# Chunked attention and a two-layer MLP on one core: 35 instructions exchange places, q is loaded before v, and the last tile's products are split in halves

## The chip, the cores and the metric

The kernel runs on one NeuronCore of a Trainium2 chip. The core has five engines, each with its own instruction stream that runs strictly in order: PE (TensorE: matmuls, with weight loads shown apart as PEld), DVE (VectorE), ACT (ScalarE), POOL (GpSimd) and SP (SyncE, which here only issues DMAs). They wait for each other through semaphores. The metric is the device time of one execution in microseconds (us).

## The reference

```python
q, k, v: (8, 8, 576, 64) float32            # batch, heads, sequence, head size
scores = scale * q_c @ k_c.T                # in chunks of 64 positions
attn = exp(scores - max); attn /= sum + 1e-9
x = (attn @ v_c) -> (4608, 512)             # tokens x model
h = x @ w_in                                # (512, 2048)
out = max(0.01 * h, h) @ w_out              # (2048, 512), float32
```

## The kernel before

**Tiles.** The 4608 tokens are 36 *units* of 128 tokens (u = 0..35) and 9 *tiles* of 512 tokens (j = 0..8). Unit u's attention makes 128 columns of x, transposed, in `xT`; four units feed one tile of the MLP. Matmuls take fp16 and accumulate in float32 in the eight PSUM banks.

**A unit's attention**, by the names of its tasks and the lines of their instructions:

- load of q and k (L1877, POOL's DMA queue). For the units up to 11 PE transposes them (tq, tk: L2095) and ACT or DVE copies the result to SBUF (q0, q1, k: L1959 on ACT, L1961 on DVE). For the later units SP issues a DMA transpose (L2116) and p0, p1 copy (L1959, L1961).
- s: scores on PE (L2164). m: row maxima (L2170) and b: subtraction (L2173) on DVE. x: exponential on ACT (L2177); h for unit 25. z: row sums on DVE (L2189); ze: + 1e-9 on POOL or DVE (L2192); zi: reciprocal on DVE (L2195); n: product with it on POOL or DVE (L2198).
- e: transpose on PE (L2224) and c: its copy; from unit 20 on d: a DMA transpose (L2232). v: product with v on PE (L2242). a: copy into `xT` on ACT or DVE (L1959, L1961).

**First layer of tile j.** Tiles 0 and 1 are done plainly: L1.j... on PE (L2322) and g, the leaky ReLU, on ACT (L2299). The others use Strassen's scheme with seven products instead of eight, in four parts n = 0..3: xs0.j to xs3.j are sums of blocks of `xT` and fi0 to fi3 sums of blocks of w_in (DVE, L2269); Q1.j.n to Q7.j.n are the products (PE, L2373, four matmuls of 256 columns each). Between them p5.j.n and y.j.n copy out of PSUM or from bank to bank (L1959 or L1961), z.j.n and w.j.n add on DVE (L2398, L2401), and c11, c12, c21, c22 are the leaky ReLU on ACT (L2299). A unit's z has one number behind it, a tile's z has two.

**Second layer of tile j.** Seven products again: S1.j.h to S3.j.h are sums of blocks of the first layer's result (DVE, L2441), S4.j.h.0 a later one (L2536), fo0 to fo3 sums of w_out. P1.j.p0, P1.j.p1 to P7 are the products of the two halves of 128 tokens (PE, L2495, eight matmuls of 256 columns each), in the order P1, P2, P6, P5, P7, P4, P3 as far as their keys go. cp1, cu2, cu3 and d21 copy (L1959 or L1961), d11, d22, d12 add (DVE, L2512) into `osb`, and SP stores (st). P5 and P3 accumulate in one bank, and d22 reads it between them. Tile 8's chain is done for each half apart; its second half has P3 in two parts of 128 columns (L2567) in that same bank, with an add (L2572) and a store (L2557) for each.

**The first loads.** Unit 0's q, k and v come through the hardware queues as whole float32 blocks: v_f and then q_f are issued on SP, k_f on ACT (L1923). castq and castk0, castk1 turn q and k to fp16; put0.0 to put3.0 place v's quarters (all L1959 or L1961).

**Who sets the order.** Nothing is scheduled on the chip. `Plan` (L97 to L280) holds one `Task` per instruction or group, with estimated durations, keys with hand-set offsets (`NUDGE`), buffers from rings (`RINGS`) and, where two engines can do it, a choice of engine. `Plan.run` plays this forward: each engine takes the ready task with the lowest key; buffers and PSUM banks are assigned then. The tasks' `emit` functions are collected in `order` with the planned start, sorted by it, and called in that order. So each engine's stream is the planned order, and each wait is for what was emitted before. Until 24 us idle matmuls (L2608) fill planned gaps on PE.

Of the kernel before, what the change touches and what calls it, by code (L numbers as in the profile page):

```python
# [14 lines left out]
PE, ACT, DVE, POOL, SP = "PE", "ACT", "DVE", "POOL", "SP"  # L15
# [81 lines left out]
class Plan:  # L97
# [89 lines left out]
    def fill(self, a, z, used, count, emit, order):  # L187

        n = count(a, z)
        if not n:  # L190
            return
        for i, o in enumerate(self.rings["bank"]):
            if i not in used and (o is None or not o.open and o.till <= a):
                b = Buf("bank")
                b.till = z + 0.1
                self.rings["bank"][i] = b
                self.whole[i] = False
                order.append((a, emit(n, i)))
                return

    def run(self, slack=0.04, filler=None):
        for t in self.tasks:
            t.left = len(t.deps)
            for d in t.deps:
                d.next.append(t)
        ready = self.ready = {e: [] for e in LATENCY}
        for t in self.tasks:
            if not t.left:
                self.put(t)
        now = dict.fromkeys(LATENCY, 0.75)  # L210
        now[POOL] = 1.25
        order = []
        todo = len(self.tasks)

        def behind(t, e, at):

            return self.lean.get(e, 0.0) + max(now[e], at) + t.engs[e] + sum(x.engs[e] for x in ready[e] if x.key < t.key and x.eng == e)

        while todo:
            best = None  # L220
            for e, ts in ready.items():
                can = []
                loads = []
                for t in ts:
                    if isinstance(t.after, tuple) and t.after[0] == "soft":
                        loads.append(t)
                        continue
                    p = self.place(t, e)
                    if p is None:
                        continue  # L230
                    if len(t.engs) > 1:
                        mine = behind(t, e, p[0])
                        if any(behind(t, o, p[0]) < mine - 1e-9 for o in t.engs if o != e):
                            continue
                    can.append((max(now[e], p[0]), t, p[1]))
                for t in sorted(loads, key=lambda t: t.key):
                    p = self.place(t, e)
                    if p is not None:
                        can.append((max(now[e], p[0]), t, p[1]))
                        break  # L240
                if not can:
                    continue
                first = min(c[0] for c in can)
                wait = self.hold if e in (ACT, DVE) and first < 25.0 else slack
                c = min((c for c in can if c[0] <= first + wait), key=lambda c: c[1].key)
                if best is None or c[0] < best[0]:
                    best = (*c, e)
            ends = self.dma.next()
            if ends and (best is None or ends[0] <= best[0]):
                self.land()  # L250
                continue
            if best is None:
                raise RuntimeError("stuck: " + " ".join(f"{e}:{t.name}" for e, ts in ready.items() for t in ts))
            start, t, slots, e = best
            t.eng = e
            if filler is not None and e == PE:
                self.fill(now[PE], start, [i for b, i in slots if b.ring == "bank"], *filler, order)
            for b, i in slots:
# [6 lines left out]
            order.append((start, lambda t=t: t.emit(t.eng) if len(t.engs) > 1 else t.emit()))  # L265
# [12 lines left out]
        self.now = now  # L278
        order.sort(key=lambda x: x[0])
        return [x[1] for x in order]  # L280


# [1499 lines left out]
           'P3.8.p1': -11.34,  # L1782
           'd12.8.1': 12.97,
           'st.8.1.1': -5.87,
           'st.8.0.1': -12.65},
# [5 lines left out]
 'VROW': (0, 1, 2, 3)}  # L1791

@with_exitstack
def kernel(
# [9 lines left out]
    nc = tc.nc  # L1807

    B, H, S, D = q.shape
    d_model, d_ff = moe_w_in.shape  # L1810
# [51 lines left out]
    def mem(buf):  # L1862
        return MEM[buf.ring][buf.slot]
# [563 lines left out]
    def layer2_seven(j, done):  # L2427
# [45 lines left out]
        def chain(ps_of, k0, span, shift):  # L2473
# [13 lines left out]
            def product(m, deps):  # L2487
                t = []
                opens = m in ("P1", "P2", "P5")
                for p in ps_of:  # L2490
                    def emit(p=p):
                        if opens and p == ps_of[0]:
                            ps[into[m]] = bank(bufs[into[m]], [128, n, HM])
                        for fc in range(HB):
                            nc.tensor.matmul(  # L2495
                                out=ps[into[m]][:, p - ps_of[0], :], lhsT=lhs[m][0]()[:, fc, p * 128:(p + 1) * 128], rhs=rhs[m][:, fc, :],
                                start=(opens and p == ps_of[0] and fc == 0), stop=(fc == HB - 1), skip_group_check=True,
                            )
# [28 lines left out]
            s = side(1)  # L2527
            c22 = dve("d22", "V", tmp(tu3), o(1, 1), key["P7"] + step + 0.2, P5 + [c3], [bV, tu3] + s["bufs"], s["opens"])
            P4 = product("P4", [c3])
            s4 = []  # L2530
            for h in range(2):
# [25 lines left out]
                    f"st.{j}.{name}", SP, 0.5, key["P3"], lambda: nc.sync.dma_start(out=out[r0:r0 + 128, m0:m1], in_=mem(osb[r])[:, 1, m0:m1]),  # L2557
                    deps=deps, bufs=[osb[r]], after=("hard", 0.83 * (m1 - m0) / 512, 1, 0.0))

            leave("ur", 1, HM, d_model, [c22])  # L2560
            leave("ul", 1, 0, HM, [c21])
            leave("l", 0, 0, HM, [c11])
            prev = []
            for q0 in range(0, HM, 128):
                def emit(q0=q0):
                    for fc in range(HB):
                        nc.tensor.matmul(  # L2567
                            out=ps["V"][:, 0, q0:q0 + 128], lhsT=lhs["P3"][0]()[:, fc, 128:256], rhs=rhs["P3"][:, fc, q0:q0 + 128],
                            start=False, stop=(fc == HB - 1), skip_group_check=True)

                def emit_d(q0=q0):
                    nc.vector.tensor_tensor(  # L2572
                        out=mem(osb[0])[:, 1, HM + q0:HM + q0 + 128], in0=ps["V"][:, 0, q0:q0 + 128], in1=mem(tu2)[:, 0, q0:q0 + 128], op=ADD)

                prev = [task(
                    f"P3.{j}.p1.{q0}", PE, 0.46, key["P3"] + 0.01 * q0, emit, deps=[c22] + s4 + lhs["P3"][2] + fo + prev,
                    bufs=lhs["P3"][1] + [bufs["V"]], bank="part")]
                c12 = task(f"d12.{j}.1.{q0}", DVE, 0.2, key["P3"] + step, emit_d, deps=prev, bufs=[bV, tu2, osb[0]])
                leave(f"q{q0}", 0, HM + q0, HM + q0 + 128, [c12])

        if last:
# [29 lines left out]
    for emit in plan.run(filler=(filler, emit_idle)):  # L2611
        emit()


# [28 lines left out]
```

## Time and profile before

| | us |
|---|---|
| median of 3 runs | 282.1 (282.0 to 282.23) |
| the profiled execution | 281.71 |
| its span, first to last instruction | 279.6 |
| PE's first matmul / end of its last | 1.0 / 276.0 |

The profile is of one execution, taken by the hardware. A row of the timeline shows the start and the length in us, the engine and the line, what is written and read, and the number of instructions; a bracket gives the engine's idle time before it and what ended that. Rows with SPq are DMA issues. Granted TensorE clock: 1.0 throughout.

### The profile page before, as it was taken

The numbers are of one execution on the slowest core, as the hardware profiler recorded it, in microseconds if no ns is written. First come the engines' busy times: TensorE is split into PE (matmuls) and PEld (weight loads), VectorE is DVE, ScalarE is ACT, GpSimd is POOL, SyncE is SP. The second block draws the span as 40 slices with busy tenths as digits, with TensorE's granted clock in tenths as the row PEclk, the third lists the DMA queues.
The fourth block names the chain that finished last, engine by engine and source line by source line (L and its number), as shares of the span: only waits on it lengthen the run. The fifth ranks groups of instructions, "written<-read, shape, count | busy, mean of one in ns | idle before, by whom it ended". The sixth has DMA issues, their size and how long they took to land. (4 is left out here: it accounts for less than half of the span.)

```text
span 279.6 us, 8040 instructions
## 1 busy us (share of the span) xinstructions
PE 268.0 (96%) x3249; PEld 242.6 (87%) x3249; DVE 227.3 (81%) x425; ACT 208.1 (74%) x396; POOL 139.1 (50%) x180
## 2 busy tenths in 40 slices
PE   6789999999999989999999999999999999999994
PEld 6778999999988979999889889889889888988884
DVE  5788799989989889899998999878699927734841
ACT  5987999876786899799677897476876766677431
POOL 8979598657876147254736996462334020000000
PEclk9999999999999999999999999999999999999999
DMA  9999999999999939999999999999535022100132
GB/s 147 162 178 164 164 184 193 156 131 122 147 192 180 185 76 124 144 157 175 141 171 138 138 151 173 208 154 172 150 101 108 19 40 80 75 2 0 72 149 81
DMA packets 157236, 37.09 MB, mean 133 GB/s; under 512 B 147600, under 2 KB 152848, under 8 KB 157200
## 3 DMA queue, kind: packets, MB, share of 16 engines
q0 software_dynamic: 113904, 17.96, 98.6%
q1 hardware_dynamic: 42256, 18.36, 39.0%
q8 instruction: 25, 0.41, 0.7%
q10 hardware_dynamic: 1040, 0.26, 0.4%
q14 instruction: 11, 0.09, 0.1%
HBM read 36.70 MB, written 9.44 MB: 165 GB/s over the span
## 5 line engine op out<-in xcount | busy, mean ns | idle before, releaser
L2299 ACT ACTIVATE gT<-bank 128x512 f16<-128x512 f32 x116 | 64.7, 600 | 16.3 <-PE bank L2373 14.7
L2495 PEld LDWEIGHTS <-gT 128*128 128x128 f16 x576 | 55.1, 98 | 6.8 <-issue 0.7
L2495 PE MATMUL bank<-w_outT,gT 128*128 128x256 f16 x432 | 53.7, 273 | 0.5 <-ACT u L1959 0.5
L2373 PEld LDWEIGHTS <-FI 128*128 128x128 f16 x448 | 43.0, 98 | 7.5 <-issue 2.4
L2373 PE MATMUL bank<-xs,FI 128*128 128x256 f16 x336 | 45.7, 272 | 1.5 <-DVE xs L2269 0.6
L2495 PEld LDWEIGHTS <-S 128*128 128x128 f16 x424 | 40.6, 98 | 4.8 <-DVE S L2441 0.3
L1877 POOL DMA_DIRECT2D qk<-in_q_dram x39 | 33.7, 869 | 10.1 <-PE bank L2095 5.3
L1877 POOL DMA_DIRECT2D qk<-in_k_dram x39 | 34.0, 878 | 7.8 <-DMA KT<-qk 5.6
L2495 PE MATMUL bank<-FO,S 128*128 128x256 f16 x288 | 35.7, 273 | 0.0
L2373 PEld LDWEIGHTS <-w_inT 128*128 128x128 f16 x336 | 31.9, 98 | 4.3 <-issue 0.6
L2322 PE MATMUL bank<-xT,w_inT 128*128 128x128 f16 x512 | 32.7, 219 | 0.0
L2373 PE MATMUL bank<-xT,w_inT 128*128 128x256 f16 x224 | 31.3, 273 | 0.0
L2322 PEld LDWEIGHTS <-w_inT 128*128 128x128 f16 x512 | 29.5, 98 | 0.0
L1959 ACT ACTIVATE p<-bank 128x512 f32<-128x512 f32 (+1 forms) x37 | 20.6, 586 | 11.0 <-PE bank L2495 5.5
L2198 POOL TENSOR_TENSOR en<-ex,z 128x512 f16<-128x512 f16 x18 | 20.4, 1138 | 14.6 <-DVE z L2195 5.7
L2192 POOL TENSOR_SCALAR z<-z 128x8 f32<-128x8 f32 x25 | 8.4, 336 | 38.0 <-DVE z L2189 30.7
L2189 DVE TENSOR_REDUCE z<-ex 128x8 f32<-128x512 f16 x36 | 24.4, 678 | 3.4 <-ACT ex L2177 3.1
L2177 ACT ACTIVATE ex<-sh 128x512 f16<-128x512 f32 x35 | 22.1, 631 | 6.4 <-DVE sh L2173 4.6
L2398 DVE TENSOR_TENSOR bank<-bank,p 128x512 f32<-128x512 f32 x28 | 19.0, 694 | 8.7 <-PE bank L2373 6.5
L2170 DVE TENSOR_REDUCE mx<-bank 128x8 f32<-128x512 f32 x36 | 24.4, 681 | 1.8 <-PE bank L2164 1.8
L2173 DVE TENSOR_TENSOR sh<-bank,mx 128x512 f32<-128x512 f32 x35 | 23.6, 679 | 0.5
L2401 DVE TENSOR_TENSOR w<-bank,p 128x512 f32<-128x512 f32 x28 | 18.8, 686 | 5.8 <-PE bank L2373 5.7
(83 smaller groups left out, 478.4 us busy)
## 6 DMA issues: line engine op xcount, KB each, us to landing
out_dram<-osb SPq DMA_DIRECT2D x16, 512.0 KB, 5.1
VB<-in_v_dram POOLq DMA_DIRECT2D x14, 288.0 KB, 8.5
qk<-in_k_dram POOLq DMA_DIRECT2D x31, 128.0 KB, 6.8
qk<-in_q_dram POOLq DMA_DIRECT2D x31, 128.0 KB, 8.5
w_outT<-in_moe_w_out_dram POOLq DMA_DIRECT2D x4, 512.0 KB, 10.2
w_inT<-in_moe_w_in_dram POOLq DMA_DIRECT2D x6, 256.0 KB, 6.5
qk<-in_k_dram POOLq DMA_DIRECT2D x8, 64.0 KB, 6.1
w_inT<-in_moe_w_in_dram POOLq DMA_DIRECT2D x4, 128.0 KB, 6.1
```

The costliest lines, as they stand in the source:

```text
L1877: nc.gpsimd.dma_start(out=to[a - r0:z - r0, which], in_=src[a // S, :, a % S:a % S + z - a, :].rearrange("h p d -> p h d"),)
L1959: nc.scalar.activation(out=to(), in_=of(), func=AFT.Copy, bias=0.0, scale=1.0)
L2170: nc.vector.tensor_reduce(out=mem(mx)[:, 0], in_=t["sp"], axis=AXL.X, op=ALU.max)
L2173: nc.vector.tensor_tensor(out=mem(sh), in0=t["sp"], in1=mem(mx)[:, 0].unsqueeze(2).to_broadcast((128, 8, CH)), op=ALU.subtract)
L2177: nc.scalar.activation(out=mem(ex), in_=mem(sh), func=AFT.Exp, bias=0.0, scale=SCL)
L2189: nc.vector.tensor_reduce(out=mem(z)[:, 0], in_=mem(ex), axis=AXL.X, op=ALU.add)
L2198: (nc.gpsimd if eng == POOL else nc.vector).tensor_tensor(out=mem(en), in0=mem(ex), in1=mem(z)[:, 2].unsqueeze(2).to_broadcast((128, 8, CH ...
L2299: nc.scalar.activation(out=to, in_=of, func=AFT.Prelu, bias=0.0, scale=1.0, alpha=0.01)
L2322: nc.tensor.matmul(out=t["h"][:, i, :], lhsT=w_inT[:, n, fc * 128:(fc + 1) * 128], rhs=xT[:, n, r0 % RING:r0 % RING + tb], start=(i == 0 a ...
L2373: nc.tensor.matmul(out=ps[to][:, i, :], lhsT=lhs[:, t, f:f + 128], rhs=rhs()[:, t], start=(opens and i == 0 and t == 0), stop=(t == 1), sk ...
L2398: nc.vector.tensor_tensor(out=ps["V"], in0=ps["X"], in1=mem(p5), op=ADD)
L2495: nc.tensor.matmul(out=ps[into[m]][:, p - ps_of[0], :], lhsT=lhs[m][0]()[:, fc, p * 128:(p + 1) * 128], rhs=rhs[m][:, fc, :], start=(opens ...
```

## The change

1. `Plan.run` takes a list of moves. After the order is sorted, each pair (a, b) takes task a out and puts it directly ahead of task b. Where a stood behind b, a comes earlier by one to four places on its engine; in some pairs a stood further ahead, so that others pass it. Buffers, banks and engines stay as planned.
2. The list has 36 pairs. The first puts q_f ahead of v_f on SP.
3. In the second half of tile 8, P5 is split into two products of 128 columns as P3 was, each half has a bank of its own from P5 to P3, and d22 and d12 become two adds each.

Applied one after the other, the pairs make these orders on the engines (only stretches that the prediction speaks of):

- SP: q_f, v_f.
- DVE, 28 us: q0.7, then the memset zv.1.1.1. 38 us: z.5, fi2, fi0.
- ACT, 99 us: y.2.3, a.14. PE, 102 us: Q4.2.0, e.12. DVE, 100 us: zi.12, zi.22.
- DVE, 139 us: z.4.0, z.21; then S4.3.0.0, w.4.0, and S4.3.1.0 only ahead of y.4.1.
- PE, 157 us: s.25, v.23, P4.3.p0, P5.4.p0, P4.3.p1. DVE: S3.4.1, m.25, z.26, zi.24, xs0.5, d22.3.0, xs1.5, zi.26, xs2.5, n.26.
- DVE, 195 us: b.31, xs2.6, xs3.6.
- DVE, 213 us: z.32, m.34, S1.6.1, zi.32, S2.6.1, b.34, m.35, S3.6.1, b.35. PE, 217 us: P6.6.p1, P2.6.p1, v.28, P7.6.p0.

```diff
-                order.append((a, emit(n, i)))
+                order.append((a, emit(n, i), None))
...
-    def run(self, slack=0.04, filler=None):
+    def run(self, slack=0.04, filler=None, moves=()):
...
         order.sort(key=lambda x: x[0])
+        for name, behind_it in moves:
+            x = next(x for x in order if x[2] == name)
+            order.remove(x)
+            order.insert(next(i for i, y in enumerate(order) if y[2] == behind_it), x)
         return [x[1] for x in order]
...
+ 'MOVES': (('q_f', 'v_f'),
+           ('P3.1.p0', 'Q3.2.1'),
+           ('zi.12', 'zi.22'),
+           ('a.14', 'c22.2.2'),
+           ('S3.6.1', 'b.35'),
+           ('b.34', 'm.35'),
+           ('m.34', 'zi.32'),
+           ('xs0.5', 'd22.3.0'),
+           ('z.26', 'xs0.5'),
+           ('fi2', 'fi0'),
+           ('q0.7', 'zv.1.1.1'),
+           ('w.4.0', 'S4.3.1.0'),
+           ('z.4.0', 'z.21'),
+           ('xs3.5', 'z.25'),
+           ('S4.3.1.0', 'y.4.1'),
+           ('Q5.5.3', 's.27'),
+           ('zi.24', 'xs0.5'),
+           ('xs2.5', 'n.26'),
+           ('Q4.2.0', 'e.12'),
+           ('xs3.7', 'zi.35'),
+           ('P2.6.p1', 'v.28'),
+           ('v.29', 's.34'),
+           ('P5.4.p0', 'P4.3.p1'),
+           ('P3.3.p0', 'Q1.5.1'),
+           ('L1.1.0.1.0', 'L1.1.1.2.0'),
+           ('P7.5.p0', 'P4.4.p1'),
+           ('b.31', 'xs2.6'),
+           ('c12.7.0', 'c22.7.1'),
+           ('s.32', 'Q2.6.2'),
+           ('Q6.8.0', 'P6.7.p1'),
+           ('Q1.7.2', 'P4.6.p1'),
+           ('y.5.3', 'c11.5.2'),
+           ('Q2.2.2', 'P7.1.p1'),
+           ('m.34', 'S1.6.1'),
+           ('Q3.3.3', 'e.16'),
+           ('y.2.2', 'S4.1.1.0'),)}
...
-            P5 = product("P5", [])
+            apart = n == 1 and ps_of[0] == 1
+            QS = range(0, HM, 128) if apart else ()
+            bW = [Buf("bank") for _ in QS]
+            pw = {}
+
+            def quarter(m, q0, deps):
+
+                i, opens = q0 // 128, m == "P5"
+
+                def emit():
+                    if opens:
+                        pw[i] = bank(bW[i], [128, 128])
+                    for fc in range(HB):
+                        nc.tensor.matmul(
+                            out=pw[i], lhsT=lhs[m][0]()[:, fc, 128:256], rhs=rhs[m][:, fc, q0:q0 + 128],
+                            start=(opens and fc == 0), stop=(fc == HB - 1), skip_group_check=True)
+
+                return task(
+                    f"{m}.{j}.p1.{q0}", PE, 0.46, key[m] + 0.01 * q0, emit, deps=list(deps) + lhs[m][2] + fo,
+                    bufs=lhs[m][1] + ([] if opens else [bW[i]]), opens=[bW[i]] if opens else [], bank="part")
+
+            def add(name, r, q0, by_, key, deps, bufs, opens):
+                def emit():
+                    nc.vector.tensor_tensor(
+                        out=mem(osb[r])[:, 1, HM + q0:HM + q0 + 128], in0=pw[q0 // 128], in1=mem(by_)[:, 0, q0:q0 + 128], op=ADD)
+                return task(f"{name}.{j}.1.{q0}", DVE, 0.2, key, emit, deps=deps, bufs=[bW[q0 // 128], by_] + bufs, opens=opens)
...
+                c22 = [add("d22", 1, q0, tu3, key["P7"] + step + 0.2, P5[q0] + [c3], s["bufs"], s["opens"]) for q0 in QS]
...
+            for q0 in QS:
+                P3 = quarter("P3", q0, [c22[q0 // 128]] + s4)
+                c12 = add("d12", 0, q0, tu2, key["P3"] + step, [P3], [osb[0]], [])
                 leave(f"q{q0}", 0, HM + q0, HM + q0 + 128, [c12])
```

More of the change, by code (lines that the diff above doesn't have):

```diff
@@ L264, in run @@
             now[e] = t.end
-            order.append((start, lambda t=t: t.emit(t.eng) if len(t.engs) > 1 else t.emit()))
+            order.append((start, lambda t=t: t.emit(t.eng) if len(t.engs) > 1 else t.emit(), t.name))
             for o in t.engs:
@@ L1784 @@
            'st.8.1.1': -5.87,
-           'st.8.0.1': -12.65},
+           'st.8.0.1': -12.65,
+           'P5.8.p1.0': 46.8,
+           'P5.8.p1.128': 46.8,
+           'P3.8.p1.0': -11.34,
+           'P3.8.p1.128': -11.34,
+           'd22.8.1.0': 4.69,
+           'd22.8.1.128': 4.69,
+           'd12.8.1.0': 12.97,
+           'd12.8.1.128': 12.97},
  'RINGS': {'osb': 3, 'qk': 5, 'QZ': 2, 'KT': 6, 'QT': 4, 'et': 5, 'p5': 3},
@@ L2523, in chain @@
             c2 = act("cu2", "X", tmp(tu2), key["P6"] + step, P6, [bX], [tu2])
-            P5 = product("P5", [])
+            apart = n == 1 and ps_of[0] == 1
[19 more added lines that the diff above has]
+                return task(f"{name}.{j}.1.{q0}", DVE, 0.2, key, emit, deps=deps, bufs=[bW[q0 // 128], by_] + bufs, opens=opens)
+            if apart:
+                P5 = {q0: [quarter("P5", q0, [])] for q0 in QS}
+            else:
+                P5 = product("P5", [])
             P7 = product("P7", [c2])
             c3 = act("cu3", "X", tmp(tu3), key["P7"] + step, P7, [bX], [tu3])
-            s = side(1)
-            c22 = dve("d22", "V", tmp(tu3), o(1, 1), key["P7"] + step + 0.2, P5 + [c3], [bV, tu3] + s["bufs"], s["opens"])
+            if apart:
+                s = side(1)
+                c22 = [add("d22", 1, q0, tu3, key["P7"] + step + 0.2, P5[q0] + [c3], s["bufs"], s["opens"]) for q0 in QS]
+            else:
+                s = side(1)
+                c22 = dve("d22", "V", tmp(tu3), o(1, 1), key["P7"] + step + 0.2, P5 + [c3], [bV, tu3] + s["bufs"], s["opens"])
             P4 = product("P4", [c3])
@@ L2558, in leave @@
                     deps=deps, bufs=[osb[r]], after=("hard", 0.83 * (m1 - m0) / 512, 1, 0.0))
-            leave("ur", 1, HM, d_model, [c22])
+            leave("ur", 1, HM, d_model, c22)
             leave("ul", 1, 0, HM, [c21])
             leave("l", 0, 0, HM, [c11])
[L2563 to L2578, printed above, removed]
+            for q0 in QS:
+                P3 = quarter("P3", q0, [c22[q0 // 128]] + s4)
+                c12 = add("d12", 0, q0, tu2, key["P3"] + step, [P3], [osb[0]], [])
                 leave(f"q{q0}", 0, HM + q0, HM + q0 + 128, [c12])
@@ L2609, in emit_idle @@
         return go
-    for emit in plan.run(filler=(filler, emit_idle)):
+    for emit in plan.run(filler=(filler, emit_idle), moves=KNOBS.get("MOVES", ())):
         emit()
```

2 lines of the change are left out of this document (1 added, 1 removed).

## The prediction

> **What bounds the kernel now.** I read the busy times first.
>
> ```profile
> PE 268.0 (96%) x3249; PEld 242.6 (87%) x3249; DVE 227.3 (81%) x425; ACT 208.1 (74%) x396; POOL 139.1 (50%) x180
> ```
>
> PE (TensorE) is busy for 268.0 of 279.6 us, so exchanging instructions can win at most the 11.6 us in which it is idle. The table by stretches says where those are.
>
> ```profile
> 0.00:30.00 30.00, 24.70 (x407) 22.62 (x408) 21.75 (x53) 22.62 (x43) 26.67 (x39) 1.00 1.73 163
> ```
> ```profile
> 230.00:280.00 50.00, 45.98 (x447) 41.20 (x444) 26.12 (x47) 25.54 (x49) 0.00 (x0) 1.00 0.18 64
> ```
>
> The columns are stretch, length, then PE, PEld, DVE, ACT and POOL busy with instructions, granted clock, DMA share, GB/s. PE idles 5.3 us in the first 30, 4.0 us in the last 50 (nearly all behind the last product), and so 2.3 us in the 200 us between. There it stops only in short stalls. The chain of waits shows the last of these (start, length, what):
>
> ```profile
> 217.97 0.63 ACT ex L2177
> 218.60 0.49 ACT u L1959
> 219.10 0.04 issue
> 219.14 1.03 PE bank L2495 x8
> 220.17 7.00 PE bank L2373 x64
> ```
>
> From 219.14 the chain is PE to the last product. The last row gives PE's pace: 7.00 / 64 = 0.109 us for a product of 256 columns. A row's own length is longer, because matmuls overlap; so I measure a stall as the start of the waiting product less the start of the one before it plus 0.109 us for each of its matmuls. It is then a little longer than the idle time in the row's bracket.
>
> **The change part by part.** Moves add and remove no work. A move is worth the stall that it ends, less the stall that it opens.
>
> *219 us.* P7.6 waits for cu2.6, a copy on ACT (line 1959).
>
> ```profile
> 217.62 1.04 PE L2495 MATMUL bank<-w_outT,gT 128*128 128x256 f16 x8
> ```
>
> PE was free at 217.62 + 8 x 0.109 = 218.49 and began P7.6 at 219.14: a stall of 0.65. By the chain the copy stood behind x.34 (ACT ex), which waited for b.34 on DVE. The change puts m.34 and b.34 ahead of S3.6.1, so x.34 is over before cu2.6's input exists. S3.6.1, which P7.6 also reads, takes b.34's place behind m.34, b.34 and m.35; it is done no later than b.34 is now, before x.34 begins at 217.97, and so ahead of 218.49. **-0.65.**
>
> *The load of q first.* SP issues v_f's DMA, then q_f's.
>
> ```profile
> 1.25 0.57 SPq L1923 DMA_DIRECT2D u<-in_q_dram  x1
> ```
> ```profile
> 6.69 0.63 ACT L1959 ACTIVATE qk<-u 128x512 f16<-128x512 f32 x1 [2.23 <-DMA u<-in_q_dram]
> 7.34 0.41 ACT L1959 ACTIVATE S<-p 64x256 f16<-64x256 f32 x1
> 7.81 0.59 ACT L1959 ACTIVATE QZ<-bank 64x512 f16<-64x512 f16 x1
> ```
> ```profile
> 9.14 0.40 PE L2095 MATMUL bank<-ident,qk 128*128 128x128 f16 x4 [0.59 <-DVE qk L1961]
> ```
>
> The second of the two lands just before 6.69. After the change that one is v. The cast of q (6.69) then goes early, but the next instruction in ACT's order, put2.0 (7.34), reads v: it starts near 6.69, not earlier. Behind it stand q1.0 (7.81), then q0.0 and castk0 on DVE, then tk.0 on PE (9.14) and all of unit 0. So of ACT's 2.23 us of waiting for q only 7.34 - 6.69 = 0.65 comes out at the end of this chain. Bounds: 0, if v lands 0.65 later than q did; 2.2, the whole wait, if v lands with q. I take the row at which v's place in the queue is now filled. **-0.65.** It lasts only if the next loads are there 0.65 earlier too (second rival).
>
> *q0.7 ahead of a memset.*
>
> ```profile
> 27.57 0.30 DVE L1977 MEMSET VB<- 64x288 uint32 x1
> 27.90 0.42 DVE L1961 COPY QZ<-bank 64x512 f16<-64x512 f16 x1
> ```
> ```profile
> 29.67 0.39 PE L2164 MATMUL bank<-KT,QZ 128*128 128x64 f16 x8 [0.24 <-ACT gT L2299]
> ```
>
> ACT waits for this copy, does q1.7 and then g.0.0.0, which frees the bank that s.7 opens at 29.67. All of it starts 27.90 - 27.57 earlier: **-0.33.** The memset's reader is far off.
>
> *fi2 behind z.5.* e.5 waits for n.5 on POOL.
>
> ```profile
> 42.89 0.40 PE L2224 MATMUL bank<-ident,en 128*128 128x128 f16 x4 [0.22 <-POOL en L2198]
> ```
>
> z.5 goes ahead of a long sum, but its input x.5 ends behind n.4, so DVE waits a little; n.5 still meets fi1. Between -0.4 (the stall with what the bracket hides) and +0.4: I take **+0.1.**
>
> *Around 100 us.* Q6.2.3 waits for y.2.3, ahead of which a.14 goes away; e.12 waits for n.12.
>
> ```profile
> 99.69 1.03 PE L2373 MATMUL bank<-xs,FI 128*128 128x256 f16 x8 [0.56 <-ACT bank L1959]
> ```
> ```profile
> 101.73 0.40 PE L2224 MATMUL bank<-ident,en 128*128 128x128 f16 x4
> 101.96 0.60 PE L2373 MATMUL bank<-xs,w_inT 128*128 128x256 f16 x4
> ```
> ```profile
> 100.76 0.69 DVE L2401 TENSOR_TENSOR w<-bank,p 128x512 f32<-128x512 f32 x1
> ```
>
> The earlier y.2.3 does not come through: w.2.0 (100.76) is behind z.2.0 and n.22 on a full DVE, and Q4.2.0 needs it. Q4.2.0, now ahead of e.12, can start at 101.45 + 0.04, e.12 follows, and what came behind Q4.2.0 starts 0.23 + 0.44 later, at 102.16 in place of 102.40. **-0.24**; between 0 and -0.6, the whole first bracket.
>
> *140 us.* z.4.0 and w.4.0 each go ahead of one DVE instruction.
>
> ```profile
> 138.00 1.91 PE L2495 MATMUL bank<-FO,S 128*128 128x256 f16 x16
> 140.08 0.60 PE L2373 MATMUL bank<-xs,FI 128*128 128x256 f16 x4 [0.16 <-DVE bank L2398]
> ```
> ```profile
> 141.82 0.60 PE L2373 MATMUL bank<-xT,w_inT 128*128 128x256 f16 x4
> 142.47 0.60 PE L2373 MATMUL bank<-xs,w_inT 128*128 128x256 f16 x4
> ```
>
> The stalls are 140.08 - 139.74 = 0.34 and 142.47 - 142.26 = 0.21, each shorter than the instruction of about 0.6 that is passed. What is passed (z.21, S4.3.1.0) has readers microseconds later. **-0.55**, or 0 if DVE brings the wait back.
>
> *160 us.* Q5.5.2 waits for xs0.5.
>
> ```profile
> 156.96 1.04 PE L2495 MATMUL bank<-FO,S 128*128 128x256 f16 x8
> 157.84 0.40 PE L2242 MATMUL bank<-et,VB 128*128 128x64 f16 x8
> 158.07 1.91 PE L2495 MATMUL bank<-FO,gT 128*128 128x256 f16 x16
> 160.61 0.27 PE L2373 MATMUL bank<-xs,FI 128*128 128x256 f16 x1 [0.62 <-DVE xs L2269]
> ```
> ```profile
> 157.01 0.59 ACT L1959 ACTIVATE u<-bank 128x512 f32<-128x512 f32 x1
> ```
> ```profile
> 159.55 1.00 DVE L2269 TENSOR_TENSOR xs<-xT 128x512 f16<-128x512 f16 x1
> 160.48 0.41 DVE L2269 TENSOR_TENSOR xs<-xT 128x512 f16<-128x512 f16 x1
> ```
> ```profile
> 159.23 1.04 POOL L2198 TENSOR_TENSOR en<-ex,z 128x512 f16<-128x512 f16 x1
> ```
>
> The stall is 160.61 - 159.81 = 0.80. xs0.5 goes ahead of d22.3.0, to 159.0, and so ahead of POOL's n.24; alone such a sum takes 0.41. But P5.4.p0 (156.96) is also moved, between P4.3's two halves. v.23 then takes its place and ends at 157.19, and P4.3 must wait for cu3.3.0 on ACT until 157.60: a **new stall of 0.43** that P5.4.p0 covered, with P5.4.p0, P4.3.p1 and Q5.5.2 queued behind it. **-0.37**, between +0.1 and -0.8.
>
> One page speaks against this place. The Trainium skill, "SBUF — State Buffer", Who interferes with whom, says that a DVE instruction with two SBUF inputs and a POOL instruction that reads SBUF exclude each other, and that the first to issue blocks the other. The trace agrees: xs0.5 began behind n.24 and took 1.00. By that rule this term is -0.37 if xs0.5 issues first and about nothing if n.24 does.
>
> *199 us.* b.31 goes ahead of two sums; x.31, p5.6.1, z.6.1 and Q7.6.1 hang on it.
>
> ```profile
> 198.43 0.60 PE L2373 MATMUL bank<-xT,w_inT 128*128 128x256 f16 x4
> 199.10 0.38 PE L2373 MATMUL bank<-xs,FI 128*128 128x256 f16 x2
> ```
>
> 199.10 - 198.87 = **-0.23**, or 0.
>
> *The last products by halves.* P5 and P3 get a bank for each half; the matmuls cost the same.
>
> ```profile
> 276.02 0.49 DVE L2572 TENSOR_TENSOR osb<-bank,u 128x128 f32<-128x128 f32 x2 [1.27 <-PE bank L2567]
> ```
> ```profile
> 276.34 0.33 SPq L2557 DMA_DIRECT2D out_dram<-osb  x1
> 276.76 0.38 SPq L2557 DMA_DIRECT2D out_dram<-osb  x1
> ```
>
> Now both adds wait until P3's second half is done, and two stores then queue on SP. With its own bank the first half's add and store run under the second half, and the last store goes in the slot of the first: 276.76 - 276.34 = **-0.42.** Nothing lies behind it. The cost is one more add for d22, covered by P4 (0.87 on PE).
>
> The other moves meet stalls of about 0.1 or none. I set their gains against new waits like P5.4.p0's, and count neither.
>
> The sum: 0.65 + 0.65 + 0.33 - 0.10 + 0.24 + 0.55 + 0.37 + 0.23 + 0.42 = 3.34. The profiled execution took 281.71 (span 279.6 and 2.1 around it), the median is 282.1, 0.4 above. 282.1 - 3.3 = **278.8 us.**
>
> **The rivals.**
>
> *The waits come back one place further on.* Against a full gain: DVE is 81% busy on the mean; a product that is early finds the next sum unfinished. For the gain: DVE's own idle times there are waits for PE, which shrink with it. If the terms at 28, 100, 140, 160 and 199 us (1.72) are lost, 1.62 is left: 280.5.
>
> *The loads hold the start.*
>
> ```profile
> DMA  9999999999999939999999999999535022100132
> ```
>
> The DMA engines have work nearly all the time until slice 14. If landings, not PE, set the pace there, what is won before 30 us (0.65 + 0.33) is lost again: 279.8. Against it: units wait microseconds behind their loads.
>
> *Slower: DVE and POOL fall out of step.* Every move shifts which of DVE's two-input sums meets a POOL instruction. The price is 1.00 - 0.41 = 0.59 each (the rows at 160 us). It decides when more than 3.34 / 0.59, so six, new meetings stand directly before a product that waits; with eight the time is 278.8 + 4.7 = 283.5. Against it: POOL works only half the time, and between 30 and 230 us few stalls end on such a sum. The rule behind it is that of the Trainium skill, "SBUF — State Buffer", Who interferes with whom; the price is the rows'.
>
> *The order does not do what it says:* a wait on an engine's count may still cover the instruction that was passed, as both last adds now wait for the second half. For the last tile that costs 0.42: 279.2, inside the forecast.
>
> **How the numbers follow.** Forecast 0.63 (with the fourth rival), waits that return 0.19, loads 0.12, slower 0.04, about no change 0.02. About 0.2% (0.56 us) is what a measurement can tell from no change. Faster 0.94, same 0.02, slower 0.04. The low end adds to 3.34 the 0.43 of the new stall, 0.5 if e.5's wait goes, 0.4 of the first bracket at 100 us and 0.2 of the bounds of q's load: 277.2. The high end takes in most of the first rival: 280.7.
>
> **What would show it.** Right: tk.0 near 8.5; no idle before Q7.4.0, Q4.4.0, Q7.6.1 and P7.6; a new idle before P4.3 at about 157 less the shift; d12's first add beginning under P3's second half. Wrong: put2.0 not at v's landing; the same brackets one product later; sums of 1.0 us in new places.

## The result, and the profile after

The changed kernel took 278.19 us (median of 4 runs, 277.98 to 278.58), the kernel before 282.17 on the same chip (4 runs, 282.0 to 282.3): a ratio of 0.9863, interval 0.9848 to 0.9878. The forecast was 278.8 in a range of 277.2 to 280.7. The profiled execution is the slowest of the four, 278.58 with a span of 276.6; against the profile of before (281.71, 279.6) that is 3.1 less, between the medians 4.0. The two differ because the profile of before is of a faster execution than its median and this one is of the slowest; where executions of one kernel differ, the experiments show in part.

The busy times, first view of the page of the changed kernel:

```profile
PE 267.6 (97%) x3257; PEld 242.9 (88%) x3257; DVE 226.7 (82%) x426; ACT 207.9 (75%) x396; POOL 139.1 (50%) x180
```

No work went away (eight matmuls and one add more, from the halves). TensorE's idle time went from 11.6 us to 9.0. Where it went, the table by stretches shows (columns as in the prediction), cut at the start of P1.0.p0, the first product of tile 0's second layer, and at the start of P3's second half, the last product. Before:

```profile
30.00:58.11 28.11, 27.89 (x531) 27.73 (x528) 26.71 (x43) 26.23 (x51) 20.83 (x27) 1.00 2.00 174
58.11:275.37 217.26, 214.80 (x2311) 191.78 (x2309) 178.34 (x328) 159.15 (x305) 91.56 (x116) 1.00 1.28 124
275.37:279.60 4.23, 0.61 (x11) 0.44 (x8) 0.49 (x2) 0.14 (x1) 0.00 (x0) 1.00 0.29 93
```

After:

```profile
0.00:30.00 30.00, 25.37 (x416) 23.19 (x417) 22.97 (x54) 23.18 (x43) 26.36 (x39) 1.00 1.75 165
30.00:57.94 27.94, 27.48 (x522) 27.30 (x520) 26.39 (x43) 25.58 (x50) 19.93 (x26) 1.00 1.99 168
57.94:272.67 214.73, 214.11 (x2320) 192.00 (x2318) 176.70 (x329) 158.97 (x305) 92.78 (x117) 1.00 1.29 126
272.67:276.60 3.93, 0.61 (x11) 0.43 (x8) 0.58 (x2) 0.13 (x1) 0.00 (x0) 1.00 0.32 100
```

The second column is the length. The **middle** went from 217.26 to 214.73, 2.53 less; the **end** from 4.23 to 3.93, 0.3 less; the **start** only from 58.11 to 57.94, 0.17 less, though the forecast had put 0.88 there (0.65 + 0.33 - 0.10).

In the middle the waits that the prediction wanted to end are gone; Q6.2.3, from which it took nothing, still stalls for 0.45 (0.73 before). Where the chain of waits had its last stall, with ACT's ex and u, it now reads:

```profile
211.08 5.24 PE bank L2543 x48
216.55 0.87 PE bank L2543 x8
217.43 7.00 PE bank L2421 x64
```

It runs on TensorE alone now. The timeline at Q7.4.0, Q4.4.0 and Q7.6.1 (start, length, what; an idle time would stand in a bracket) has no bracket left:

```profile
139.15 0.60 PE L2421 MATMUL bank<-xs,FI 128*128 128x256 f16 x4
...
141.34 0.60 PE L2421 MATMUL bank<-xs,w_inT 128*128 128x256 f16 x4
...
197.06 1.47 PE L2421 MATMUL bank<-xs,FI 128*128 128x256 f16 x12
```

The start went as forecast, and then not. tk.0 is at 8.30 (9.14 before), and 0.63 to 0.64 of that holds up to v.2, the product at 22.56 (23.19 before). Then come these two rows, L1.0.0.1.0 and e.3:

```profile
23.43 0.34 PE L2370 MATMUL bank<-xT,w_inT 128*128 128x128 f16 x3 [0.31 <-DMA w_inT<-in_moe_w_in_dram]
...
27.55 0.40 PE L2272 MATMUL bank<-ident,en 128*128 128x128 f16 x4 [0.36 <-ACT QZ L2007]
```

The first waits for loadQ.2.1, which landed at 23.39 (at 22.71 before). The second had no bracket before; e.3 stood at 27.51 then, so nothing of the gain was left there. q0.7's place gave 0.5 back at s.7 (29.20, 29.67 before), and e.5 took 0.25 of that (its stall is 0.63, 0.38 before).

At the end the first half's add starts at 272.87, under the second half's product, which began at 272.67 and ends at 273.28. This is as planned:

```profile
272.22 1.06 PE L2585 MATMUL bank<-w_outT,S 128*128 128x128 f16 x16
...
272.87 0.29 DVE L2595 TENSOR_TENSOR osb<-bank,u 128x128 f32<-128x128 f32 x1 [1.03 <-PE bank L2585]
273.31 0.29 DVE L2595 TENSOR_TENSOR osb<-bank,u 128x128 f32<-128x128 f32 x1 [0.15 <-PE bank L2585]
```
```profile
273.25 0.38 SPq L2639 DMA_DIRECT2D out_dram<-osb  x1
```
```profile
273.73 0.40 SPq L2639 DMA_DIRECT2D out_dram<-osb  x1
```

From the end of the last matmul (273.28) to the start of the last store (273.73) 0.45 us pass; before, 276.76 - 275.98 = 0.78.

### The profile page after: what moved, and what is told of

The parts are those of the page before. It is cut to its first block, busy times and chain, and to the rows that moved or that the text cites. A ratio compares the mean times of both kernels' runs of the same rounds, so it can differ in the third digit from the quotient of the medians.

```text
span 276.6 us, 8050 instructions
## 1 busy us (share of the span) xinstructions
PE 267.6 (97%) x3257; PEld 242.9 (88%) x3257; DVE 226.7 (82%) x426; ACT 207.9 (75%) x396; POOL 139.1 (50%) x180
## 4 chain that ended last, share of the span: by engine, by line
PE 81%; DMA 9%; POOL 5%; ACT 1%; DVE 1%; issue 1%; POOLq 0%
PE bank L2543 38%; PE bank L2421 30%; PE bank L2370 6%; DMA VB<-in_v_dram 4%; DMA w_inT<-in_moe_w_in_dram 3%; PE bank L2290 3%; PE bank L2212 2%; DMA qk<-in_k_dram 2%; POOL qk L1925 2%; PE bank L2272 1%; POOL xs L2093 1%; PE bank L2143 1%; PE bank L2585 1%; DVE xs L2317 1%; ACT ex L2225 0%
## 5 line engine op out<-in xcount | busy, mean ns | idle before, releaser
L2543 PEld LDWEIGHTS <-S 128*128 128x128 f16 x416 | 39.7, 98 | 4.7 <-DVE S L2489 0.3
L2543 PE MATMUL bank<-FO,S 128*128 128x256 f16 x280 | 34.8, 273 | 0.0
L2240 POOL TENSOR_SCALAR z<-z 128x8 f32<-128x8 f32 x25 | 7.5, 301 | 32.7 <-DVE z L2237 26.7
L2007 ACT ACTIVATE xT<-bank 128x512 f16<-128x512 f32 x36 | 21.2, 599 | 3.0 <-PE bank L2290 2.8
```

Of the source, the lines that this page charges most:

```text
L2007: nc.scalar.activation(out=to(), in_=of(), func=AFT.Copy, bias=0.0, scale=1.0)
L2543: nc.tensor.matmul(out=ps[into[m]][:, p - ps_of[0], :], lhsT=lhs[m][0]()[:, fc, p * 128:(p + 1) * 128], rhs=rhs[m][:, fc, :], start=(opens ...
```

## The experiments

Theory going in: each stall on TensorE is a term of its own, and the terms add up. Rivals: landings of loads set the pace before 60 us; a removed wait comes back one place further on. All times are medians; each ratio is against the kernel before on the same chip, whose median was 281.9 to 282.2. Starts and stalls are worked out as in the prediction, each from one profile of the kernel in question. The medians of the kernels that have most of the moves lie between 277.96 and 279.24, and most of their intervals overlap; so what a single move is worth is read from the traces.

**The halves alone.**

```
-         'MOVES': (('q_f', 'v_f'), ... ),}
+         'MOVES': ()}
```

> The changed kernel without any of its 36 moves: only the last tile's products by halves are left. Theory (the end is a step of its own, nothing upstream of it matters): every product up to the last starts when it did before, and from the end of the last matmul to the start of the last store 0.45 to 0.36 us pass in place of 0.78, so the time is 0.33 to 0.42 us under that of before, about 281.8. Rival (the order does not do what it says, a wait on a count still covers what was passed): 0.78 stays and the time is 282.2.

281.61, ratio 0.9986 (0.9975 to 0.9996), 0.38 under the kernel before. From the last matmul to the last store 0.45 passes, as in the changed kernel. The theory holds at its lower end: by the trace the halves are worth 0.33.

**Only the moves with a term of their own.** The list of moves is cut to these:

```
+ 'MOVES': (('q_f','v_f'), ('a.14','c22.2.2'), ('S3.6.1','b.35'), ('b.34','m.35'), ('m.34','zi.32'),
+           ('xs0.5','d22.3.0'), ('fi2','fi0'), ('q0.7','zv.1.1.1'), ('w.4.0','S4.3.1.0'),
+           ('z.4.0','z.21'), ('Q4.2.0','e.12'), ('P5.4.p0','P4.3.p1'), ('b.31','xs2.6'))}
```

> The changed kernel with 13 of its 36 moves, those that the forecast gave a term of their own (q_f, q0.7, fi2, a.14, Q4.2.0, z.4.0, w.4.0, xs0.5, P5.4.p0, b.31, b.34, S3.6.1 and the first move of m.34), and the halves. Theory of the forecast (the other 23 are worth nothing together): the time of the full change, 278.2 within 0.3. Rival read from the two traces (y.2.2 and Q2.2.2 are worth 0.20 at 88 us, two more places 0.07 and 0.06): 278.5. Second rival (the 23 guard against waits that the 13 open): 279 or more.

279.2, ratio 0.9899 (0.9883 to 0.9915): the second rival. From P1.0.p0 to the last product it takes 215.96, against 214.73 with all moves and 217.26 with none. So the thirteen are worth 1.30 there, and the other 23 another **1.2**. The places differ by 0.35 at 89 us, 0.27 at Q4.4.0, 0.15 at v.20 just behind it and 0.39 from there to Q2.5.1, with a small rest. In the last of these one sees how a small move works. s.27 waits for p0.27, a copy on POOL, in this run:

```profile
159.07 1.47 PE L2398 MATMUL bank<-xs,FI 128*128 128x256 f16 x12
160.01 0.65 POOL L1986 COPY QZ<-QT 64x512 f16<-64x512 f16 x1
160.72 0.41 PE L2189 MATMUL bank<-KT,QZ 128*128 128x64 f16 x8 [0.17 <-POOL QZ L1986]
160.96 0.60 PE L2398 MATMUL bank<-xs,FI 128*128 128x256 f16 x4
```

TensorE is free at 159.07 + 12 x 0.109 = 160.38 and loses 0.34. The product behind it, Q5.5.3 (160.96), could have gone; one of the 23 moves puts it ahead of s.27, and in the changed kernel s.27 (160.65) has no bracket.

**The old order of q's and v's loads.**

```
- 'MOVES': (('q_f', 'v_f'),
+ 'MOVES': (
```

> The changed kernel, with v's load ahead of q's on SP as it was before; the other 35 moves stay. Theory of the forecast (the 0.65 won at tk.0 goes through to the end): tk.0 at 9.1 in place of 8.3, and 278.85. Rival (the loads set the pace until 24 us): tk.0 is 0.8 later, but L1.0.0.1.0, which waits for loadQ.2.1's landing, starts within 0.2 of the changed kernel's 23.43, and the time is 278.2 to 278.4.

278.7, ratio 0.9889 (0.9871 to 0.9906). tk.0 is at 9.14, v.2 at 23.20, 0.64 behind the changed kernel; L1.0.0.1.0 at 23.59 is 0.16 behind it, as the rival says, and e.3 stands where it did. But later this execution lost 0.45 at e.5 and another 0.5 at tq.8:

```profile
54.92 0.40 PE L2142 MATMUL bank<-ident,qk 128*128 128x128 f16 x4 [0.37 <-DMA qk<-in_q_dram]
```

From P1.0.p0 (58.96) to the last product it takes 214.72, the changed kernel's 214.73. So the middle repeats to 0.01, and what is uncertain lies before 58 us. The time decides nothing: 278.7 is what neither side said, and the changed kernel itself has 278.19 in one set of runs and 278.53 in another (next).

**The changed kernel again.**

> The changed kernel itself once more, on the chip on which the next three run, so that they can be set against it. Expected: 278.2, and from 60 us on the same starts relative to each other as in its first profile (P1.0.p0 to the last product within 0.05), while the stalls before 60 us differ by some tenths, as those of kernels with the same order there did.

278.53, ratio 0.9881 (0.9865 to 0.9896). On this chip the change is worth 3.4 (281.91 to 278.53), in the first set of runs 4.0; its five executions lie between 277.99 and 279.15, and the profiled one is the fastest of them. The middle takes 214.85, 0.12 more, where 0.05 was expected (all between Q2.5.1 and P2.5.p0). The start is 0.7 shorter than in the first profile of the very same program. P1.0.p0 in the first profile and in this one:

```profile
57.94 0.82 PE L2543 MATMUL bank<-w_outT,gT 128*128 128x256 f16 x6
```
```profile
57.23 0.82 PE L2543 MATMUL bank<-w_outT,gT 128*128 128x256 f16 x6
```

Two waits make the difference. L1.0.0.1.0 has none:

```profile
22.96 0.61 PE L2370 MATMUL bank<-xT,w_inT 128*128 128x128 f16 x8
```

And e.3 is at 26.88 in place of 27.55. In both profiles it starts 0.05 after n.3's end on DVE (27.50 and 26.83). The bracket of the first names ACT's copy q0.5, which ended at 27.50 too; but in the second q0.5 ends at 27.20, behind e.3's start, so it isn't what e.3 needs. n.3 hangs on ze.3, a sum of 128x8 on DVE that was caught behind a DMA issue of POOL's in the first profile:

```profile
24.55 1.16 POOL L1937 DMA_DIRECT2D VB<-in_v_dram  x1
24.86 0.85 DVE L2240 TENSOR_SCALAR z<-z 128x8 f32<-128x8 f32 x1
25.70 0.89 POOL L1925 DMA_DIRECT2D qk<-in_k_dram  x1
```

and slipped in just behind the start of the next issue in the second:

```profile
23.56 1.16 POOL L1937 DMA_DIRECT2D VB<-in_v_dram  x1 [0.21 <-issue]
24.70 0.89 POOL L1925 DMA_DIRECT2D qk<-in_k_dram  x1
24.87 0.17 DVE L2240 TENSOR_SCALAR z<-z 128x8 f32<-128x8 f32 x1
```

Of the kernel before such a pair exists too: the halves alone have its order up to there, and e.3 is at 27.99 (ze.3 took 0.62) against 27.51 (0.17).

So against the one profile of before the start is worth 58.11 - 57.94 = 0.17 by the first profile and 58.11 - 57.23 = **0.88** by the second. That the second is the forecast's 0.88 is chance: in the profile of the halves alone, which has the order of before, P1.0.p0 is at 58.59, and against that the two give 0.65 and 1.36.

**Can the start's gain be held by order?** Three runs. In all three n.5 is issued before zi.5, so it reads the reciprocals that an earlier unit left in the same buffer (unit 7, by the planned buffers) in place of unit 5's; e.5's wait for zi.5 is then missing from their times. To the changed kernel's list the first adds:

```
+           ('loadQ.2.1','loadQ.4.1'), ('loadQ.4.1','loadk.7'), ('zi.3','zv.1.1.0'), ('n.3','zv.1.1.0'),
+           ('q1.5','zv.1.1.3'), ('q0.5','zv.1.1.3'), ('n.5','loadq.11'),
```

> The changed kernel and seven further moves at the three stalls that gave the start's gain back: loadQ.2.1 and loadQ.4.1 exchange places in POOL's order (L1.0.0.1.0's stall of 0.47); zi.3 and n.3 go ahead of two memsets on DVE, q1.5 and q0.5 ahead of one on ACT (e.3's stall of 0.53); n.5 goes ahead of loadq.11's issue on POOL (e.5's stall of 0.63). Theory (these waits, and not PE's work, swallowed what q's early load had won): 1.3 to 1.6 less, 276.7; L1.0.0.1.0 near 23.0, e.3 near 26.7, e.5 near 41.0. Rival (the DMA engines, busy nearly all the time, hold the next products instead): the waits come back at tq.5, tq.7, tq.4 or s.6, and 277.6 or more.

278.97, ratio 0.9896 (0.9876 to 0.9915). L1.0.0.1.0 at 22.67, e.3 at 26.40 and e.5 at 41.69 are all early, the last by 1.0 against the first profile. By e.6 it is gone:

```profile
45.84 0.83 PE L2377 MATMUL bank<-xT,w_inT 128*128 128x128 f16 x12 [0.40 <-DVE sh L2228]
```

L1.1.1.2.0 waits for b.6, which stands on DVE behind the long sum fi3. With 0.32 more two products on, e.6 is at 49.86 (49.83 in the changed kernel). The rival's time came, but its reason was wrong: DVE's order, not a landing. The second run adds:

```
+           ('zv.1.1.0','q1.4'), ('zv.1.1.2','q1.4'), ('zv.1.1.1','q1.4'),
+           ('loadq.11','loadq.10'), ('loadk.15','loadq.13'), ('m.6','fi3'), ('b.6','fi3'),
```

> The changed kernel with fourteen further moves before 60 us: loadQ.2.1 and loadQ.4.1 exchanged; zi.3 and n.3 on DVE and q1.5 and q0.5 on ACT ahead of memsets, three memsets of DVE behind c.3; n.5 ahead of loadq.11 on POOL; m.6 and b.6 ahead of fi3 on DVE; loadk.15 and loadq.11, whose readers are microseconds off, behind loads that are read at once. Theory (the last run lost its 1.0 us to DVE's memsets and to fi3 ahead of m.6, and not to the DMA engines): Q1.2.0 at 80 us starts 0.8 to 1.4 earlier than in the changed kernel, and the time is 276.8 to 277.4. Rival (the landings set the pace until 60 us whatever the order): the gain is at most 0.3 at Q1.2.0, and waits for landings stand in its place.

278.75, ratio 0.9885 (0.9871 to 0.9898). With b.6 out of the way the wait stands at e.6, for n.6 on DVE, behind S1.0.0 and S2.0.0:

```profile
49.77 0.40 PE L2286 MATMUL bank<-ident,en 128*128 128x128 f16 x4 [0.70 <-DVE en L2260]
```

Q1.2.0 is at 80.08, against 80.20 and 79.47 in the two profiles of the changed kernel, so the theory's 0.8 to 1.4 did not come; nor is there a landing in their place, as the rival has it. Neither list is faster than the changed kernel, which took 278.53 on the chip of the second.

The same kernel with v's load first (the edit of the old order of the loads):

> The run before with v's load ahead of q's, as before the change. Theory (with the later waits out of the way q's early load is worth its full 0.65): 0.65 later than the run before at L1.0.0.1.0, at Q1.2.0 and at the end. Rival (the loads take it back): 0.3 to 0.65 at L1.0.0.1.0, 0.2 or less at Q1.2.0 and at the end.

279.24, ratio 0.9903 (0.9889 to 0.9916). It is behind the run before by 0.62 at v.2 and at L1.0.0.1.0, 0.26 at e.3, 0.56 at P1.0.p0, 0.49 at the last product and 0.49 in the medians. The executions of the two do not overlap (278.47 to 278.88 and 279.07 to 279.36). So in this kernel q's early load is worth about half a microsecond to the end. At L1.0.0.1.0 both sides allowed 0.62; at the end the rival's 0.2 is passed and the theory's 0.65 not quite reached, so the theory is nearer.

**P5.4.p0 where it was,** in the changed kernel.

```
-           ('P5.4.p0', 'P4.3.p1'),
```

> The changed kernel with P5.4.p0 left where it was, ahead of P4.3. Theory of the forecast (that move opens a stall at P4.3.p0 and wins nothing): P4.3.p0's stall of 0.19 goes, Q5.5.2 stays without a stall, so 0.2 less from there to the end. Rival (P5.4.p0 behind P4.3.p0 lets xs0.5 and d22.3.0 be in time): Q5.5.2 waits 0.2 to 0.4 and the end is the same or up to 0.2 later. Both: within 0.3 of the changed kernel's time, to be read from the starts in the trace.

278.65, ratio 0.9882 (0.9868 to 0.9896). The middle takes 214.53, P4.3.p0's stall of 0.19 is gone, and Q5.5.2 has none: in this profile the move costs 0.2, as the forecast's mechanism says.

**Waits one by one:** the second of the three lists above, with P5.4.p0 where it was, n.5 behind zi.5 again, and z.6's chain moved.

```
-           ('P5.4.p0', 'P4.3.p1'),
-           ('n.5','loadq.11'),
+           ('z.6','S1.0.0'), ('ze.6','S2.0.0'), ('zi.6','S2.0.0'), ('n.6','S2.0.0'),
```

> The changed kernel without P5.4.p0's move and with sixteen others before 60 us: those of the run with fourteen, but n.5 stays behind zi.5 and only loadq.11 goes out of its way, and z.6, ze.6, zi.6 and n.6 go ahead of S1.0.0 and S2.0.0 (e.6's stall of 0.86 in that run). Theory (each of these waits was DVE's or POOL's order, not a landing): no stall over 0.2 between 30 and 60 us, Q1.2.0 at 79.1 to 79.5 and 0.2 more won at Q5.5.2; the time 277.3 to 277.8, against 278.5 of the changed kernel on the last chip. Rival (the waits come back one place further, now at tq.8, fo0 or P1.0.p0, or at a landing): Q1.2.0 at 79.9 or later, and no time but the 0.2 at Q5.5.2 is won.

278.77, ratio 0.9885 (0.9872 to 0.9899). e.6's stall is gone and Q1.2.0 is at 79.67, but e.5 still stalls for 0.47, and at Q5.5.2, where 0.2 should be won, 0.66 is lost. So neither theory nor rival came out. In both places a sum on DVE and one on POOL meet; for Q5.5.2 the rows stand further down, under the three edits. At e.5, loadq.11's issue no longer stands ahead of n.5, so n.5 now meets the long sum fi1 almost from its start:

```profile
40.02 1.23 DVE L2333 TENSOR_TENSOR FI<-FI,w_inT 128x2048 f16<-128x2048 f16 x1
40.24 1.90 POOL L2262 TENSOR_TENSOR en<-ex,z 128x512 f16<-128x512 f16 x1 [1.30 <-DVE z L2259]
```

In the changed kernel it met only fi1's last 0.3:

```profile
40.53 1.17 DVE L2317 TENSOR_TENSOR FI<-FI,w_inT 128x2048 f16<-128x2048 f16 x1
41.41 1.20 POOL L2246 TENSOR_TENSOR en<-ex,z 128x512 f16<-128x512 f16 x1
```

Without such a meeting it takes 1.04 (in the first of the runs that tried to hold the start). An issue of 0.94 taken out of the way won 0.16. (Another 0.27 is lost at Q2.4.1, which waits for y.4.1 on DVE; why was not followed up.)

**Two later stalls.** Five moves are added to the list before:

```
+           ('p5.2.0','xs1.2'),
+           ('Q1.2.3','P3.1.p1'), ('y.2.3','c12.2.1'), ('z.12','d12.1.0'), ('Q2.2.3','Q7.2.0'),
```

> The run before and five further moves: p5.2.0 ahead of xs1.2 (Q5.2.2's stall of 0.28 and P6.1.p0's of 0.17 at 82 us), Q1.2.3 ahead of P3.1.p1, y.2.3 ahead of c12.2.1, z.12 ahead of d12.1.0 and Q2.2.3 ahead of Q7.2.0 (Q6.2.3's stall of 0.46 at 98 us). Theory (stalls whose input waits only for its place in the order add up): 0.3 to 0.45 won at 83 us and 0.3 to 0.45 at 99 us. Rival (DVE is full there): what is won at 99 us is lost at Q7.2.0, Q4.2.0 or v.12, within 5 us.

278.4, ratio 0.9876 (0.9855 to 0.9897). At 82 us 0.46 is won. At 98 us Q6.2.3's stall goes, 0.45, and comes back larger within 3 us:

```profile
99.45 0.60 PE L2442 MATMUL bank<-xs,FI 128*128 128x256 f16 x4 [0.27 <-DVE bank L2467]
99.88 0.60 PE L2442 MATMUL bank<-xT,FI 128*128 128x256 f16 x4
100.94 0.60 PE L2442 MATMUL bank<-xs,w_inT 128*128 128x256 f16 x4 [0.46 <-DVE w L2470]
```

Q7.2.0 and Q4.2.0 wait for z.2.0 and w.2.0 on DVE; the place ends 0.27 behind. Theory at the first place, rival at the second.

**fi2 as before,** in the changed kernel.

```
-           ('fi2', 'fi0'),
```

> The changed kernel with fi2 ahead of z.5 again, as before the change. Theory of the forecast (z.5's place costs or wins 0.1): e.5's stall is 0.5 to 0.6, against 0.63. Second theory (n.5 waits for loadq.11's issue on POOL, which takes its 0.94 us whenever the queue gets to it): e.5's stall is 0.63 again within 0.05, or 0.38 as before the change if loadq.11 is issued earlier without fi2's move. Nothing after 45 us changes but by the shift of this place.

278.43, ratio 0.9869 (0.9852 to 0.9885). e.5's stall is 0.74: a value that neither theory had. Three profiles with fi2's move have 0.63 there, but one has 0.76 (P5.4.p0 where it was) and one 1.07 (the old order of q's and v's loads), so what fi2's move is worth is not shown. The stall has another reason (below).

**Three edits together,** in the changed kernel.

```
-           ('P5.4.p0', 'P4.3.p1'),
+           ('p5.2.0','xs1.2'), ('loadk.15','loadq.13'),
```

> The changed kernel with three edits that the earlier runs point to: P5.4.p0 stays where it was (0.2 won at Q5.5.2 in one run), p5.2.0 goes ahead of xs1.2 (0.46 won at 82 us in another), loadk.15 goes behind loadv.2.1 so that loadq.8 lands earlier (a wait of 0.5 at tq.8 in two). Theory: 0.6 to 0.7 less than the changed kernel from P1.0.p0 to the end, so 214.1 us from the start of P1.0.p0 to that of the last product in place of 214.7, no wait at tq.8, and 277.6 to 278.0. Rival (without P5.4.p0's move xs0.5 can meet n.24 on POOL, as it did in two runs at a price of 0.66): Q5.5.2 waits, 214.8 and 278.4.

277.96, ratio 0.9849 (0.9829 to 0.9870). tq.8 does not wait and 0.46 is won at 82 us, but Q5.5.2 stalls for 0.67 and the middle takes 214.74: the rival, though the time is the theory's. xs0.5 and n.24 in this run, and in the changed kernel:

```profile
156.69 1.53 DVE L2318 TENSOR_TENSOR xs<-xT 128x512 f16<-128x512 f16 x1 [0.18 <-ACT xT L2008]
156.87 1.05 POOL L2247 TENSOR_TENSOR en<-ex,z 128x512 f16<-128x512 f16 x1
```
```profile
157.51 0.38 DVE L2317 TENSOR_TENSOR xs<-xT 128x512 f16<-128x512 f16 x1
157.95 1.05 POOL L2246 TENSOR_TENSOR en<-ex,z 128x512 f16<-128x512 f16 x1
```

With P5.4.p0 behind P4.3.p0, v.23 comes a place earlier, xs0.5's input with it, and xs0.5 is over before n.24 starts. Without, it escaped in one run (0.41, where that was the only edit) and was caught in the three others (1.52 to 1.53). So the move pays 0.2 to be safe from 0.66. Whether this kernel is faster than the changed one is open: the intervals overlap. With p5.2.0 ahead of xs1.2 *and* P5.4.p0's move kept it was not run.

## Why the prediction was right, step by step

- *219 us, 0.65:* 0.64 between the starts ahead of it and P7.6 (2.11 to 2.75). Right.
- *q's load, 0.65:* put2.0 went to v's landing (6.57), and 0.63 arrived at v.2. Right up to there. How much is left at 58 us differs from execution to execution; at the end about 0.5 of it was seen, in a kernel with fourteen more moves.
- *q0.7, 0.33:* v.3 starts 0.05 later than before and s.7 0.47 earlier, so 0.52 was won between them. The mechanism is right, the size too small: s.7's whole stall went, 0.40, which the forecast took as 0.33 from the copy's start.
- *fi2, +0.1:* e.5 lost 0.25. The step reasoned with z.5's place in DVE's order. The runs show that n.5 is set by POOL (loadq.11's issue, then fi1 beside it): TensorE came 0.47 earlier to s.6, n.5 ended only 0.22 earlier, and the difference is the stall. So the sign and the place were right and the reason was not.
- *100 us, 0.24:* 0.24. *140 us, 0.55:* 0.53. *199 us, 0.23:* 0.24. Right.
- *160 us, 0.37:* 0.60. The new stall at P4.3.p0 is there, for the reason given (cu3.3.0 on ACT), at 0.19 in place of 0.43 (0.41 by the forecast's own two times, 157.60 - 157.19): cu3.3.0 itself came 1.45 earlier, more than TensorE. That the move also keeps xs0.5 away from n.24 was not seen as a link; the prediction had both facts in one paragraph and priced them apart.
- *The halves, 0.42:* 0.33. The store got the first one's slot on SP, but then its own add, ending at 273.60, was last.
- *The other moves, nothing:* the step that was most mis-sized. They are worth 1.2, and the thirteen alone 1.30 in the middle, where the forecast's terms make 0.24 + 0.55 + 0.37 + 0.23 + 0.65 = 2.04. New waits took 0.74 of it, the small moves gave that back and 0.5 more. To set gains against new waits was the right balance to draw; only its result was not nothing. That the middle as a whole came within 0.5 of the forecast is in part luck: a loss of 0.74 and a gain of 1.23, neither of them counted, stand against each other.
- *At most the idle time can be won:* this bound was too tight. The last 50 us of the table reach past the end of the span, 279.6; so TensorE idled 3.6 there and not 4.0, and 2.7 in the 200 us between and not 2.3. And a stall is longer than its bracket. In the middle TensorE idled 2.46 before and 0.62 after, yet 2.53 was won; by the starts, the stalls of 0.08 and more add up to 4.8 before and 2.2 after.

The sum: middle 2.53 for 2.04, end 0.33 for 0.42, start 0.17 to 0.88 for 0.88. In the profiled execution the excess and the loss nearly cancel (3.1 for 3.3), which is luck too; the medians have 4.0 in the first set of runs and 3.4 in the second. Starts that differ as those of the profiles do would be enough for this, but the starts of the other executions were not seen.

Of the rivals, the loads did hold the start in some executions: by 0.47 at L1.0.0.1.0 in the first profile and 0.63 in that of fi2 as before, and by 0.4 to 0.6 at tq.8 in three (the old order of the loads, P5.4.p0 where it was, fi2 as before). In the second profile neither wait is there, so this is scatter and not a bound. The waits that come back are seen in the experiments at almost every place that was pushed further, and in the thirteen moves alone; in the whole change the small moves hide them. The slower case needs new meetings of DVE and POOL right ahead of many products. In the changed kernel's first profile one product waits for such a meeting (ze.3, with a DMA issue), in the experiments two more, at 0.66 (xs0.5) and 0.86 (n.5, 1.90 - 1.04); the price was about right, the count far off. Meetings that no product waits for did change, both ways: in that profile eight of DVE's two-input sums are 0.35 to 0.85 shorter than before and five are 0.27 to 0.60 longer. The last rival, that the order does not do what it says, did not come: the first of the last two adds starts under the second half's product.

## What to carry to other kernels

A stall read as one start less the other at the engine's pace is worth what it says, if its input waits only for its place in a queue; price also the neighbour that is pushed back, since here thirteen such moves lost a third of their sum until others mended it. Where instructions of two engines exclude each other, a move is also a change of who meets whom: look at the pair before and after. And compare stretches, not spans: here 215 of 277 us repeat within 0.12, while the first 58 of one program differ by 0.7.

## What the runs showed of the hardware

- **A DMA issue on POOL holds up a small sum on DVE.** The TENSOR_SCALAR of 128x8 takes 0.15 to 0.17 alone. Of ze.3 in the 14 profiles nine took 0.17, one 0.19 and four 0.51 to 0.85. In these four it started 0.27 to 0.44 us into an issue and ended with it to 0.01 us (25.71 and 25.71 in the rows above). In seven the issue was only 0.00 to 0.17 us old, and the sum went through; why is not shown. In the other three the issue had 0.2 us or less to go. The Trainium skill, "SBUF — State Buffer", Who interferes with whom, lists tensor_scalar among the operations that can take the pair of ports shared with GpSimd and then exclude it. The rows agree in that the sum and the issue do exclude each other; whether ze.3 takes that pair is not shown.
- **Two-input sums on DVE and on POOL do exclude each other, and the price is about what is left of the other one.** xs0.5 took 0.37 to 0.41 free. When n.24's end was 0.72, 0.91 and 1.23 us away at its start, it took 1.00, 1.20 and 1.52, so about 0.1 less than that time was lost. n.5 took 1.04 free, 1.20 when fi1 had 0.3 to go and 1.90 when it had 1.0 to go. The same section of the Trainium skill has it that the first to issue blocks the other. With fi1 and n.5 that holds; with xs0.5 and n.24 the trace shows xs0.5's start 0.18 ahead of n.24's, and yet it is xs0.5 that waits, while at a lead of 0.23 it went through in 0.41. Whether the recorded start is the issue that counts was not tried.
- **The stretch with the loads scatters, the rest hardly.** The start of P1.0.p0 lies between 57.23 and 58.38 in five profiles of the changed kernel or of one that differs from it by one move or three (57.94, 57.23, 57.82, 58.38, 57.30), and at 58.11 and 58.59 in two with the order of before. Landings are one cause: loadQ.2.1 landed at 23.39 and 21.90 in the two profiles of the changed kernel. ze.3's meeting with a DMA issue is another.
